# Half-height matmuls two at a time: scores and the last 64 rows of the low halves

## The chip, the cores and the metric

One core of a Trainium2 chip. The metric is the device time of one execution in microseconds (us). The kernel before took 1639.52 us, the median of three runs (1639.21 to 1640.65). Engines are named as in the profile: PE is TensorE's matmuls and PEld its weight loads, DVE is VectorE, ACT ScalarE, POOL GpSimd, SP the engine that issues the DMAs.

## The reference

The input x has 2048 rows of 576 columns. Two branches are mixed by a gate per row:

```
g = sigmoid((x * gate_w).sum(-1, keepdims=True))
a = infini_attention(x)              # 32 heads of 18 columns, 4 segments of 512 rows
b = (gelu(x @ w_gate) * (x @ w_up)) @ w_down     # hidden width 4608
out = g * a + (1 - g) * b
```

In a segment, each head has causal softmax attention over its 512 rows (`logits = q @ k.T * 18**-0.5 + mask`), mixed by a per-head sigmoid with a linear-attention memory of the segments before (`phi(q) @ M / (phi(q) @ z)`), and the result goes through `wo`. Everything is float32.

## The kernel before

**Precision.** A float32 matrix is scaled and split into two float16 parts, a high half and the low half that is left. A product is then three matmuls that add up in float32: high by high, high by low, low by high. The contraction of 576 is four chunks of 128 rows and a rest of 64. In the rest, the 64 rows of x stand twice, their high half in one half of the 128 partitions and the low half in the other, and the rows of the weights stand in both. So two full-height matmuls do the rest (`rest`, L1029 to L1032): the weights' high half by x's halves, and the weights' low half by x's halves.

**Two parts.** The projection part (0 to about 230 us) forms q, k, v and the memory's results, and leaves q and k in DRAM. Then 72 steps follow, two for each of the 36 tiles of 128 hidden columns of `w_gate` and `w_up`. The function `step(v)` writes one step out by hand in the order in which every engine executes it: nothing is scheduled later. A step does for one tile f = v // 2 and two of the four segments (c and e):

- the gate and up products of both segments, by a Strassen-like scheme with seven products instead of eight. They add up in the PSUM banks V, X (tagged G) and Y (tagged U); `product` issues six matmuls of 512 columns, `rest` two. `first_product` forms V, DVE copies V and X out and into Y, and the sums A11, A22, S1 to S4 and the rests G4 and U4 complete the gate and up values in turn;
- `gelu` on ACT, the multiplication by the up part on DVE (`hidden`), the split of the result into halves on ACT and POOL (`hidden_pair`);
- eight chains of the down product of the block before (`down`, L983, six matmuls of 288 columns each), into two PSUM banks tagged dn in turn; DVE adds each to the sum `acc` in SBUF (L991). A block is four steps, two tiles;
- attention of one head, in two units of one segment each, two steps behind (k = v - 2, for 64 steps): the scores (`score_piece`, L887) as matmuls of 512, 128, 384 and 256 columns into the two banks tagged st, the masking with a row maximum on DVE (L893), `powers` on ACT, `pair_rows` on ACT and POOL, a transposing DMA (`turn_rows`), and `values` (20 matmuls of 37 columns) in the next step;
- the weights of later tiles: scaling, sums and low halves on POOL (`scale_g`, `sums_g`, `low_g`, L250 to L283), high halves on ACT, the sums of squares that give the scales on DVE (`squares`, L80), and once a block `scales`, a small TensorE sum into a dn bank and six small DVE instructions.

q has two halves and k two halves too. A head's scores are one matmul with 72 rows (18 columns by four products of halves). Two 512-row loads per operand, repeated, lay these 72 rows out (`load_head`).

What sets the order around the change is the text of `step` alone: each engine executes its instructions in that order, and waits where a bank or a tile isn't free or ready.

## Time and profile before

| what | us |
|---|---|
| median of the runs | 1639.52 |
| the profiled execution | 1635.53 |
| its span in the trace | 1633.8 |
| PE busy | 1621.4 |
| DVE busy | 1268.9 |
| POOL busy | 1162.5 |
| ACT busy | 1081.3 |

The span is the time from the first instruction of the program to the last; the execution's own time is a little longer. In a row of the timeline the columns are the start and the duration in us, the engine, the line of the kernel, the operation, the tiles (out<-in), the shape (partitions x columns; 64*128 is a matmul that takes 64 of TensorE's 128 rows), the count, and in brackets the idle time before the row with what ended it. A row can merge like instructions that follow each other. In a row of a line or a tile three durations in ns stand for the shortest, the median and the longest. The mean granted TensorE clock was 1.0.

### The profile page before, as it was taken

The page shows a single profiled execution, that of the slowest core. Times are in us where ns is not written, and L with a number is a line of the kernel's source. Part 1 is how long each engine was busy: PE and PEld are TensorE (multiplying, and loading weights), DVE is VectorE, ACT ScalarE, POOL GpSimd, SP SyncE. Part 2 cuts the span into 40 slices and gives each one's busy share as a digit, 9 for nine tenths or more (in the row PEclk, how much of TensorE's full clock was granted, in tenths as well). Part 3 has the DMA queues.
Part 4 walks back from the last instruction along what each step waited for, and adds up shares of the span by engine and source line. Part 5 has one row for each costly group of instructions (what it writes and reads, how often), then busy time and mean ns, then how long its engine had stood idle before and what let it go on. Part 6 is the DMA issues. An engine that isn't in the chain of part 4 may idle for free.

```text
span 1633.8 us, 32332 instructions
## 1 busy us (share of the span) xinstructions
PE 1621.4 (99%) x11924; PEld 986.2 (60%) x11924; DVE 1268.9 (78%) x3140; ACT 1081.3 (66%) x1774; POOL 1162.5 (71%) x1057
## 2 busy tenths in 40 slices
PE   9999999999999999999999999999999999999999
PEld 5655754555665555665555665555665556665577
DVE  6576786888888888888887888888888888876643
ACT  6566447777777777777777777777767777763200
POOL 2233647888888889797978888897879797885300
PEclk9999999999999999999999999999999999999999
DMA  6532344776867686777766676777677575645351
GB/s 246 193 120 95 134 139 87 110 132 106 137 107 134 105 129 115 139 123 118 127 111 132 109 138 112 130 116 131 126 126 132 110 132 108 125 73 127 84 131 59
DMA packets 465502, 200.57 MB, mean 123 GB/s; under 512 B 425280, under 2 KB 434496, under 8 KB 464832
## 3 DMA queue, kind: packets, MB, share of 16 engines
q1 hardware_dynamic: 465344, 198.52, 62.0%
q8 instruction: 93, 1.52, 0.4%
q14 instruction: 65, 0.53, 0.1%
HBM read 82.60 MB, written 27.26 MB: 67 GB/s over the span
## 4 chain that ended last, share of the span: by engine, by line
PE 94%; DVE 3%; DMA 1%; ACT 1%; issue 1%; POOL 0%; SPq 0%; DVEq 0%; ACTq 0%; POOLq 0%
PE dn L983 25%; PE U L1025 17%; PE V L1025 11%; PE G L1025 11%; PE st L887 4%; PE pv L937 4%; PE V L1032 4%; PE st L312 3%; PE U L1032 2%; PE G L1032 2%; PE dn L312 2%; PE st L302 2%; PE G L302 1%; PE st L531 1%; PE U L302 1%
## 5 line engine op out<-in xcount | busy, mean ns | idle before, releaser
L983 PE MATMUL dn<-paird,hh 128*128 128x288 f16 x3402 | 486.7, 286 | 0.0
L1025 PEld LDWEIGHTS <-pairg 128*128 128x128 f16 x3024 | 290.2, 98 | 276.5 <-issue 5.0
L917 POOL TENSOR_TENSOR ph<-pf,ph 128x512 f16<-128x512 f32 (+1 forms) x256 | 373.8, 1460 | 79.5 <-ACT ph L916 41.0
L983 PEld LDWEIGHTS <-hh 128*128 128x128 f16 x3456 | 337.1, 98 | 137.9 <-issue 0.3
L991 DVE SCALAR_TENSOR_TENSOR acc<-dn,ev,acc 128x288 f32<-128x288 f32 x535 | 267.4, 512 | 66.5 <-PE dn L983 63.4
L906 ACT ACTIVATE pf<-pf,mb,esc 128x512 f32<-128x512 f32 (+3 forms) x512 | 293.0, 642 | 2.9
L1010 POOL TENSOR_TENSOR hh<-gl,hh 128x512 f16<-128x512 f32 x144 | 187.6, 1303 | 135.2 <-ACT hh L1009 135.2
L893 DVE CUSTOM_DVE_ANT_0 pf<-st,mask 128x512 f32<-128x512 f32 (+3 forms) x512 | 228.8, 483 | 67.5 <-PE st L887 67.5
L1025 PE MATMUL U<-xt,pairg 128*128 128x512 f16 x864 | 210.0, 379 | 1.9 <-DVE gl L1151 1.9
L1025 PE MATMUL G<-x,pairg 128*128 128x512 f16 x864 | 210.0, 379 | 0.0
L916 ACT ACTIVATE ph<-pf 128x512 f16<-128x512 f32 (+1 forms) x256 | 184.3, 720 | 0.0
L283 POOL TENSOR_TENSOR pairg<-raw,pairg 128x512 f16<-128x512 f32 (+2 forms) x144 | 167.0, 1179 | 8.3 <-ACT pairg L279 8.3
L1015 ACT ACTIVATE gl<-gl,sc 128x512 f32<-128x512 f32 x144 | 103.4, 718 | 80.4 <-DVE gl L1165 40.5
L903 ACT ACTIVATE mb<-mx,esc 128x4 f32<-128x4 f32 x128 | 37.1, 290 | 180.3 <-DVE mx L893 180.3
L1009 ACT ACTIVATE hh<-gl 128x512 f16<-128x512 f32 x144 | 89.6, 622 | 79.3 <-DVE gl L1005 79.3
L250 POOL TENSOR_SCALAR raw<-raw,sc 128x640 f32<-128x640 f32 x72 | 137.2, 1918 | 0.0
L887 PE MATMUL st<-kt,qt 72*128 72x512 f16 (+3 forms) x512 | 111.6, 299 | 0.6 <-DVE mx L893 0.6
L1025 PE MATMUL V<-x,pairg 128*128 128x512 f16 x432 | 105.0, 379 | 0.8 <-DVE gl L1125 0.8
L1025 PE MATMUL U<-x,pairg 128*128 128x512 f16 x432 | 104.8, 378 | 0.3 <-DVE gl L1165 0.3
L1025 PE MATMUL V<-xt,pairg 128*128 128x512 f16 x432 | 105.0, 379 | 0.0
L1015 ACT ACT_TABLE_LOAD x66 | 84.7, 1283 | 23.4 <-DVE gl L1152 22.6
L1032 PEld LDWEIGHTS <-pairg 128*128 128x128 f16 x576 | 56.3, 98 | 68.0
(260 smaller groups left out, 2532.3 us busy)
## 6 DMA issues: line engine op xcount, KB each, us to landing
raw<-in_wgu_dram SPq DMA_DIRECT2D x36, 640.0 KB
rawd<-in_wd_dram SPq DMA_DIRECT2D x36, 288.0 KB
qk<-stage SPq DMA_DIRECT2D x36, 256.0 KB
qt<-qk SPq DMA_DIRECT2D x128, 72.0 KB
kt<-qk SPq DMA_DIRECT2D x128, 72.0 KB
vp<-vstage SPq DMA_DIRECT2D x16, 296.0 KB
vt<-vp SPq DMA_DIRECT2D x16, 296.0 KB
orow<-oa SPq DMA_DIRECT2D x16, 288.0 KB
```

The lines of the kernel that those rows point to most:

```text
L283: pool.tensor_tensor(spot(f, *p, 1), raw_g[f][:, p[0] : p[1]], spot(f, *p, 0), OP.subtract)
L887: pe.matmul(o[:, off : off + n], q[:, e * L + qi * P : e * L + (qi + 1) * P], kt[:, e * L : e * L + n], start=True, stop=True)
L893: dve.tensor_tensor_reduce(prob[a][:, COL[qi] : COL[qi + 1]], o[:, off : off + n], mask[:, L - n :], 1.0, -3e38, OP.add, OP.max, mx[a][:, ...
L906: act.activation(r, r, AF.Exp, bias=b[:, qi : qi + 1], scale=esc[:, 0, c : c + 1])
L916: act.activation(h[:, 0, cols], p[:, cols], AF.Copy)
L917: pool.tensor_tensor(h[:, 1, cols], p[:, cols], h[:, 0, cols], OP.subtract)
L983: pe.matmul(o[:, :NH], hh[:, a, q * P : (q + 1) * P], w[:, b, n * NH : (n + 1) * NH], start=i == 0, stop=i == 5)
L991: dve.scalar_tensor_tensor(av, o[:, :NH], ev, av, OP.mult, OP.add)
L1010: pool.tensor_tensor(hh[:, 1], t, hh[:, 0], OP.subtract)
L1015: act.activation(t, o, AF.Gelu_apprx_tanh, scale=scl[f // 2][0][:, 2 + c : 3 + c])
L1025: pe.matmul(o, w[:, i, (a + k) * P : (a + k + 1) * P], x[:, b + k], start=start and k == 0 and i == 0 and b == h, stop=k == 1 and i == 1, ...
L1032: pe.matmul(o, w[:, i, a * P : (a + 1) * P], x[:, b], start=False, stop=i == 1, skip_group_check=True)
```

## The change

The scores drop the product of the two low halves: 54 rows instead of 72. The rows are laid out twice, in partitions 0 to 53 and 64 to 117. The matmul of 512 columns is issued in the first place, those of 384 and 128 in the second, and that of 256 in the first again, all four in a row; the last one's bank is now one of the two tagged dn.

The rests of the weights' low half lose their product with x's low half, so that 64 rows are left. x's halves are laid out the other way round for odd segments, so that the two segments' matmuls stand in different halves of TensorE's rows. They are issued in pairs by `low_rests`, for V and Y in the middle of a step and for X and Y at its end, each time directly ahead of a unit's scores. In the first block (fb == 0) the full-height form stays. The rest of V's first product moves: the sum for it (UG = U4 - G4) is formed once for the weights by `sums_g` instead of for x, so `first_product` has no rest, the fourth `form_sums` and its load go, and the weight tiles are 17 instead of 16 blocks wide.

Around this the order of a step changes: the hidden multiplication of both segments moves to the head of the next step (`end_pair`), scores are taken out of PSUM in pieces later (`puts`), squares and scales move behind the first of the three late down chains, and the three late chains stand together. A third `gl` buffer is added, and a head's load is eight DMAs instead of four.

```diff
     def sums_g(f):
+        g4, u4 = r[:, 4 * P : KW], r[:, KW + 4 * P :]
...
+        pool.tensor_tensor(g4, u4, g4, OP.subtract)
...
-            for i in range(2):
-                sp.dma_start(q[2 * DH * i : 2 * DH * (i + 1)], qk[:, r0 : r0 + DH, :])
-                sp.dma_start(kt[2 * DH * i : 2 * DH * (i + 1)],
-                             qk[i : i + 1, D + r0 : D + r0 + DH, :].to_broadcast([2, DH, HT]))
+            for a in (0, 64):
+                b, d = a + 2 * DH, a + 3 * DH
+                sp.dma_start(q[a:b], qk[:, r0 : r0 + DH, :])
+                sp.dma_start(q[b:d], qk[0, r0 : r0 + DH, :])
+                sp.dma_start(kt[a:b], qk[0:1, D + r0 : D + r0 + DH, :].to_broadcast([2, DH, HT]))
+                sp.dma_start(kt[b:d], qk[1, D + r0 : D + r0 + DH, :])
...
-        PIECES = ((3,), (0, 2), (1,))
+        PIECES = (((3,), 0), ((2, 0), 64), ((1,), 0))
+        def scores(a):
...
+            for qis, r in PIECES:
+                o = bank("dn", 2) if qis == (1,) else bank("st", 2)
+                spots, off, h = [], 0, slice(r, r + 3 * DH)
+                for qi in qis:
+                    n = (qi + 1) * P
+                    pe.matmul(o[:, off : off + n], q[h, e * L + qi * P : e * L + (qi + 1) * P],
+                              kt[h, e * L : e * L + n], start=True, stop=True)
...
+        def rest(o, f, a, x, parts=(0, 1)):
             w = pair_g[f]
+            for i in parts:
+                pe.matmul(o, w[:, i, a * P : (a + 1) * P], x[:, 8], start=False, stop=i == 1, skip_group_check=True)
+        def low_rests(f, *both):
+            for (o, a, x), h in zip(both, (slice(0, 64), slice(64, P))):
+                pe.matmul(o, pair_g[f][h, 1, a * P : (a + 1) * P], x[h, 8], start=False, stop=True, skip_group_check=True)
...
+        def end_pair():
+            for g in ends:
+                hidden(*g)
+            for f, c, o, g in ends:
+                hidden_pair(f, c, g)
+            ends.clear()
...
         def step(v):
...
+            end_pair()
...
+            product(Y, f, S1, t, 0, 2)
+            rest(Y, f, G4, x2_, (0,) if fb else (0, 1))
+            if fb:
+                low_rests(f, (V, G4, x1), (Y, G4, x2_))
+            if on(k):
+                puts[2 * k] = scores(2 * k)
...
             product(Y, f, S4, x2_, 2, 6)
+            rest(Y, f, UG, x2_, (0,) if fb else (0, 1))
             some(lb, late[:1])
+            if fb:
+                gate_squares(fb, i4, 1)
+                if i4 == 1:
+                    scales(fb + 1)
+                    scales_out(fb + 1)
...
             if done is not None:
                 result_low(done)
+            some(lb, late[1:])
+            if fb:
+                low_rests(f, (X, U4, x1), (Y, UG, x2_))
+                ends.append((f, c, X, g0))
+            if on(k):
+                puts[2 * k + 1] = scores(2 * k + 1)
+            ends.append((f, e, Y, g1))
```

More of the change, by code (lines that the diff above doesn't have):

```diff
@@ L261, in spot @@
         t = flat(pair_g[f])
-        o = o * P + part * 16 * P
+        o = o * P + part * GB * P
         return t[:, o : o + b - a]
@@ L1082, in first_product @@
             product(V, f, S3, xt[p], 8, 10, True)
-            rest(V, f, G4, x16[2 * p + 1], 8)
             return V
+        ends, puts = [], {}
+        def end_pair():
[4 more added lines that the diff above has]
+            ends.clear()
         def step(v):
@@ L1111, in step @@
             if on(k - 1):
+                powers(2 * k - 1)
+                pair_rows(2 * k - 1, 0)
                 pair_rows(2 * k - 1, 1)
@@ L1117, in step @@
             weights_load(fb, i4)
-            if done is not None:
-                result_high(done)
-            x1, x2_, t = x16[c], x16[e], xt[p]
-            there = v in ahead
-            V = ahead.pop(v) if there else first_product(v)
-            X, Y = bank("G"), bank("U")
-            g1 = gl_tile()
-            dve.tensor_copy(g1, V)
-            if not there:
-                scored(2 * k, 0)
-                scored(2 * k, 1)
-            product(X, f, A11, x1, 0, 4, True)
-            dve.tensor_copy(Y, X)
-            if there:
-                scored(2 * k, 0)
-                scored(2 * k, 1)
-            if v == 0:
-                last_sum(1, 1)
-            if v == 1:
-                scale_result()
-            some(fb - 1, early[:1])
             product(V, f, A22, x2_, 0, 4)
-            rest(V, f, G4, t, 12)
-            scored(2 * k, 2)
-            if on(k):
-                powers(2 * k)
+            rest(V, f, G4, x1, (0,) if fb else (0, 1))
             product(Y, f, S2, t, 4, 6)
```

187 lines of the change are left out of this document (89 added, 98 removed).

## The prediction

> **What bounds the kernel now.** I read the page's busy shares and its chain first, then TensorE's timeline over one pair of steps, then the stretches where TensorE already changes between 128 rows and 64, then DVE and POOL around the places that the change touches.
>
> ```profile
> span 1633.8 us, 32332 instructions
> PE 1621.4 (99%) x11924; PEld 986.2 (60%) x11924; DVE 1268.9 (78%) x3140; ACT 1081.3 (66%) x1774; POOL 1162.5 (71%) x1057
> PE 94%; DVE 3%; DMA 1%; ACT 1%; issue 1%; POOL 0%; SPq 0%; DVEq 0%; ACTq 0%; POOLq 0%
> ```
>
> TensorE is busy for 99% and is 94% of the chain that ends last. So the time is the length of TensorE's stream, plus every wait newly put into it. The stream of one whole step, from one first product of V to the next:
>
> ```profile
> 811.23 1.46 PE L1025 MATMUL V<-xt,pairg 128*128 128x512 f16 x6
> 812.52 0.59 PE L1032 MATMUL V<-x,pairg 128*128 128x512 f16 x2
> 812.96 0.60 PE L887 MATMUL st<-kt,qt 72*128 72x512 f16 x3
> 813.39 1.46 PE L1025 MATMUL G<-x,pairg 128*128 128x512 f16 x6
> ...
> 817.15 0.27 PE L887 MATMUL st<-kt,qt 72*128 72x256 f16 x1
> 817.26 1.46 PE L1025 MATMUL U<-xt,pairg 128*128 128x512 f16 x6
> 818.56 0.90 PE L983 MATMUL dn<-paird,hh 128*128 128x288 f16 x6
> 819.29 1.46 PE L1025 MATMUL G<-x,pairg 128*128 128x512 f16 x6
> ...
> 830.00 1.24 PE L1025 MATMUL V<-xt,pairg 128*128 128x512 f16 x5
> ```
>
> Durations include about 0.16 us of pipeline behind the streaming (six products take 1.46, the next group starts after 1.29), so costs are differences of starts: a 512-column matmul 0.216 us (1.29/6; two take 0.43), a down chain 0.73 (818.56 to 819.29), the scores' first three matmuls 0.43 (812.96 to 813.39) and the fourth 0.11. The step is 18.77 us.
>
> **What the change removes from the stream.** Each step has eight last-64-row matmuls of 512 columns (rest): 8 x 0.216 = 1.73. After it, in blocks past the first, four stay whole and four halves go out as two pairs, one half-matmul in rows 0 to 63 and the other in 64 to 127. Scores per unit: 512 and 128+384 columns side by side, then 256 alone. Whether halves run together is in the trace, since the value rows' fifth chunk is already done so:
>
> ```profile
> 13.83 0.65 PE L517 MATMUL V<-acc,raw 128*128 128x288 f32 x2
> 14.31 0.65 PE L517 MATMUL pv<-acc,raw 128*128 128x288 f32 x2
> ...
> 15.60 0.40 PE L517 MATMUL V<-acc,raw 64*128 64x288 f32 x1
> 15.60 0.40 PE L517 MATMUL pv<-acc,raw 64*128 64x288 f32 x1
> 15.84 0.40 PE L517 MATMUL V<-acc,raw 64*128 64x288 f32 x1
> ...
> 16.18 0.51 PE L517 MATMUL G<-acc,raw 128*128 128x290 f32 x1
> ```
>
> Full-height matmuls come every 0.24 us (13.83 to 14.31 for two); a pair of 64-row ones also takes 0.24 (15.60 to 15.84), its second starting within 0.01. So I take a pair as one matmul plus 0.007. Low halves: 1.73 - (4 x 0.216 + 2 x 0.223) = 0.42 us a step. Scores: 0.54 a unit becomes 0.22 + 0.11, so 0.21 saved, 0.43 for a step's two.
>
> **What the switches cost.** Each step now enters and leaves 64-row work at two places, four switches. In the fence above the last pair should be through at 15.84 + 0.24 = 16.08, and the next 128-row matmul starts at 16.18: 0.10 lost. Going in, from f16:
>
> ```profile
> 62.00 0.29 PE L315 MATMUL U<-wv,x 128*128 128x288 f16 x1
> 62.21 0.27 PE L559 MATMUL st<-ident,phi 64*128 64x64 f32 x1
> ```
> ```profile
> 229.94 0.60 PE L1025 MATMUL V<-xt,pairg 128*128 128x512 f16 x2
> ```
>
> 288 columns stream in 0.12, so 0.09 is lost. Weights can't be loaded ahead over a switch. In f32 that shows as 0.51 instead of 0.40 in the row at 16.18, 0.11 more; in f16 two products after a switch take 0.60 instead of 0.59, 0.01 more. The bounds are thus 0.09 and 0.21; I take 0.105, because all work at the new places is f16. Four switches: 0.42 us a step. The Trainium skill (TensorEngine Tiling (Array Packing), Key Properties) says that changing the tiling mode drains TensorE; it speaks against the change without a price, and the trace agrees, with 0.09 to 0.10.
>
> Net for the 62 steps with both parts (steps 4 to 65): 0.42 + 0.43 - 0.42 = 0.43, in all 26.5 us. Steps 2 and 3 (scores alone) and 66 to 71 (low halves alone) save what their switches cost: nothing.
>
> **What the new order makes TensorE wait for.** The down chains use two banks in turn. The last three (call them l0, l1, l2) now follow each other at the end of a step, with DVE's squares or scales ordered between l0's and l1's evictions, and the fourth score matmul now takes the bank of l1. The trace has this situation once, at the end of step 69:
>
> ```profile
> 1517.95 1.79 PE L983 MATMUL dn<-paird,hh 128*128 128x288 f16 x13
> 1518.28 0.52 DVE L991 SCALAR_TENSOR_TENSOR acc<-dn,ev,acc 128x288 f32<-128x288 f32 x1 [1.29 <-PE dn L983]
> ...
> 1519.37 0.93 DVE L991 SCALAR_TENSOR_TENSOR acc<-dn,ev,acc 128x288 f32<-128x288 f32 x2
> ...
> 1520.03 0.36 PE L85 MATMUL dn<-wst,ones 128*128 128x5 f32 x2 [0.28 <-DVE acc L991]
> ```
>
> A chain's bank is free 0.76 us after its last matmul has streamed (0.16 pipeline, 0.04 to DVE, 0.51 eviction, 0.05 back).
> - Every step: l2 wants l0's bank after 0.73: 0.04. Steps of the first and fourth kind (step number mod 4 is 0 or 3): 34 x 0.04 = 1.3.
> - Second kind: the scales' sum takes a bank between l0 and l1, so l1 wants l0's bank after the sum alone (0.13, by which such a step is longer before): it waits 0.63. 17 x 0.63 = 10.7. DVE's scales then delay l1's eviction. Their price before:
>
> ```profile
> 763.53 0.51 DVE L991 SCALAR_TENSOR_TENSOR acc<-dn,ev,acc 128x288 f32<-128x288 f32 x1
> 763.64 2.27 POOL L283 TENSOR_TENSOR pairg<-raw,pairg 128x512 f16<-128x512 f32 x2
> ...
> 764.15 0.67 DVE L211 TENSOR_SCALAR z<-x,z 128x4 f32<-128x4 f32 x1
> 764.85 1.08 DVE L215 TENSOR_SCALAR pb<-z 128x4 int32<-128x4 int32 x1
> 766.04 0.51 DVE L991 SCALAR_TENSOR_TENSOR acc<-dn,ev,acc 128x288 f32<-128x288 f32 x1
> ```
> ```profile
> L211 DVE TENSOR_SCALAR z<-x,z x19: 229/668/676, 174.3 to 1511.7; 128x4 f32<-128x4 f32 x19
> L215 DVE TENSOR_SCALAR pb<-z x19: 169/1079/1081, 174.6 to 1512.0; 128x4 int32<-128x4 int32 x19
> ```
>
> From eviction to eviction 2.51 us beside POOL's L283, of which both long ones are waiting (229 and 169 ns at their shortest): 1.2 without. With 1.2 the fourth score matmul finds its bank free; with 2.51 it waits 0.49 more.
> - Third kind: squares of 640 columns lie there:
>
> ```profile
> L80 DVE CUSTOM_DVE_ANT_0 junk<-raw x69: 810/1109/1898, 170.7 to 1428.5; 128x640 bf16<-128x640 f32 x69
> ```
>
> Counted from l0's end, l1's bank is free at 1.12 + the squares, and the fourth score matmul wants it at 2 x 0.73 + 0.04 + 0.105 + 0.22 + 0.22 = 2.05: it waits for what the squares take above 0.93. Between 0 (0.81 us) and 0.97 (1.90 us).
>
> Which price holds is POOL's place then. POOL's rows:
>
> ```profile
> 775.00 3.79 POOL L250 TENSOR_SCALAR raw<-raw,sc 128x640 f32<-128x640 f32 x2
> 778.77 1.72 POOL L287 TENSOR_SCALAR rawd<-rawd,sc 128x576 f32<-128x576 f32 x1
> ...
> 781.89 1.16 POOL L1010 TENSOR_TENSOR hh<-gl,hh 128x512 f16<-128x512 f32 x1
> 783.01 1.64 POOL L917 TENSOR_TENSOR ph<-pf,ph 128x768 f16<-128x768 f32 x1
> 784.62 2.27 POOL L283 TENSOR_TENSOR pairg<-raw,pairg 128x640 f16<-128x640 f32 x2
> 786.85 1.28 POOL L295 TENSOR_TENSOR paird<-rawd,paird 128x576 f16<-128x576 f32 x1
> ...
> 792.50 0.73 POOL L270 TENSOR_TENSOR raw<-raw 128x256 f32<-128x256 f32 x1
> ```
>
> In the new order the even unit's scores stand 6 us before a step's end, and POOL gets their probabilities last; with evictions, powers and copies ahead I estimate that it ends them 5 us into the next step. Behind them it does the hidden halves (2 x 1.16), the weights, the odd probabilities (1.16 for 512 columns, as for the hidden halves, + 1.64) and the low halves. l0 streams until 18.35 - 1.47 (l1, l2) - 0.76 (switches, pair, scores) = 16.1 us into its step, and DVE comes to the scales or squares 0.63 later, at 16.8. Second kind: 5.0 + 2.3 + 3.6 (sums: four of 0.73 and more, and the new one) + 2.8 + 2.5 = 16.2, clear of the scales. Third kind: 5.0 + 2.3 + 3.8 + 1.7 + 2.8 + 2.3 + 1.3 = 19.2, beside the squares. First kind: 5.0 + 2.3 + 3.8 + 2.8 + 2.3 = 16.2, clear. So I take 1.2 for the scales, and for third-kind squares 1.37, near the middle of their bounds: 0.44 x 15 = 6.6.
>
> Waits: 1.3 + 10.7 + 6.6 = 18.6 us, between 12 (no contention) and 48 (all at the long prices: 17 x 1.12 and 31 x 0.95).
>
> **What lies beside other work.** POOL gets one more subtraction and 128 more low-half columns for each of 36 weight tiles, about 0.37 + 0.26 us, 23 us on an engine with 470 us free; ACT some 4 us. A head's load is eight DMAs instead of four and half as many bytes again; the tiles are two steps ahead of use, and SP holds no work due sooner. The four form_sums of the last rows and their load go from the projection part, where TensorE is full: nothing. TensorE needs the transposed probabilities 11.9 us into the next step by the stream's order, POOL's part ends at 5: that leaves some 7 us for two transposes. A third gl buffer covers hidden halves that now end later; without it DVE's copy of U would wait for POOL. Start-up (steps 2 to 4) moves either way by up to 3 us: I take 0.
>
> **Sum.** -26.5 + 18.6 = -7.9 us. The profiled execution took 1635.5 us (span 1633.8): 1627.6 by it. The runs' median is 1639.5, 4.0 above: 1631.6 as a median.
>
> **Rivals.**
> 1. Slower, by DVE's place at the step's end: squares and scales run at the long prices because POOL is later than I count. Waits 48, so +21: 1661. For it: 19 scales had a median of 0.67 and 1.08. Against: POOL's sum ends before them in three kinds of four. It decides once waits pass 26.5 us.
> 2. Halves overlap only in part, or not (then the change doesn't do what it says). There are 264 pairs (68 x 2 and 128); the gain is gone at 0.03 us more for each, and without overlap 56 us come back: 1688. For it: the trace shows pairs in f32 alone, which streams half as fast. The Trainium skill (TensorE: Matmul & The Clock Gate, Measured speedup vs the span model) measured 3.07 for four row tiles of 512 columns; as an estimate, that efficiency would make a pair 0.28 us and the time 1647. No row shows it.
> 3. Switches cost 0.20 as in f32: 280 x 0.095 = 27 more, 1658. Against: the f16 row at 229.94.
> 4. Waits hidden (DVE ahead, banks free): only 26.5 less the small ones: 1614. For it: in the trace of before TensorE waits hardly at all. Against: three chains on two banks are a sum of rows.
>
> **How the numbers follow.** Forecast (waits of 14 to 23 us, 1627 to 1636) 0.38; rival 4 and its neighbourhood 0.20; between them and no change, within 0.2% (3.3 us, about what a measurement tells from no change) 0.14; rival 1 0.16, rival 2 0.06 (in part 0.04), rival 3 0.06. Faster 0.58, same 0.14, slower 0.28. The range goes from 1612 (rival 4) to 1660 (rivals 1 and 3, rival 2 by the estimate); the forecast's own is 1627 to 1636.
>
> **What would show it.** Pairs: U beginning within 0.01 us of V, next group 0.22 later. Switches: 0.10 between the stream's end and the next weights. Steady steps of 18.35 us in the first and fourth kind, 19.1 in the second, 18.9 in the third. TensorE waiting on DVE's acc eviction at a down chain and at the fourth score matmul. Wrong if starts of a pair lie 0.1 or more apart, or if those waits sum to over 26 us.

## The result, and the profile after

The changed kernel takes 1738.22 us (median of 5 runs, 1737.41 to 1739.14) against 1639.21 us before (5 runs): the ratio is 1.061, with a 95% interval from 1.059 to 1.062. It is 6% slower; the forecast was 1631.6.

The page of the changed kernel, its span, busy shares and the chain that ended last:

```profile
span 1736.5 us, 32603 instructions
PE 1631.3 (94%) x11924; PEld 942.7 (54%) x11924; DVE 1292.3 (74%) x3136; ACT 1089.8 (63%) x1770; POOL 1166.1 (67%) x1093
PE 51%; POOL 26%; ACT 10%; DVE 9%; issue 3%; DMA 0%; SPq 0%; POOLq 0%; DVEq 0%
```

Before, TensorE was busy for 99% and made up 94% of the chain. Now it stands still for 105 us, and 26% of the chain is POOL's. The view of TensorE's waits (who waited for what: us in total, times, longest) names them:

```profile
PE dn L982 <- POOL paird L301: 48.3, 16, 3.1
PE dn L982 <- DVE acc L990: 17.2, 30, 0.7
PE dn L982 <- DVE mx L892: 16.4, 16, 1.3
PE dn L884 <- DVE acc L990: 10.8, 14, 0.8
```

The first row is once per block (15 steps of the fourth kind and one in the start-up): a down chain waits for POOL to write the low half of the down weights (`low_d`, L301). TensorE's timeline at the end of a step of the fourth kind (step number mod 4 is 3) shows where; columns as before, idle time ahead of a row in brackets:

```profile
851.85 0.65 PE L982 MATMUL dn<-paird,hh 128*128 128x288 f16 x4
855.43 2.53 PE L982 MATMUL dn<-paird,hh 128*128 128x288 f16 x14 [2.93 <-POOL paird L301]
857.89 0.61 PE L1034 MATMUL G<-x,pairg 64*128 64x512 f16 x1
857.90 0.60 PE L1034 MATMUL U<-x,pairg 64*128 64x512 f16 x1
...
859.08 1.25 PE L1022 MATMUL V<-xt,pairg 128*128 128x512 f16 x3
```

And POOL's timeline at the same place:

```profile
847.24 1.72 POOL L293 TENSOR_SCALAR rawd<-rawd,sc 128x576 f32<-128x576 f32 x1
848.92 2.76 POOL L916 TENSOR_TENSOR ph<-pf,ph 128x512 f16<-128x512 f32 x2
851.64 2.50 POOL L289 TENSOR_TENSOR pairg<-raw,pairg 128x640 f16<-128x640 f32 x2
854.11 1.27 POOL L301 TENSOR_TENSOR paird<-rawd,paird 128x576 f16<-128x576 f32 x1
```

The late chain l0 starts with four matmuls that use ready weights, its fifth wants the low half at 852.3, and POOL ends L301 at 855.4. POOL isn't idle ahead of it; the instruction stands last in its queue. Behind the wait TensorE is also slower for a while: the pair at 857.89 takes 0.61 and 0.60 us instead of 0.39. The windows' last three columns are granted clock, DMA share and GB/s:

```profile
842.00:857.00 15.00, 12.07 (x92) 7.11 (x91) 8.98 (x22) 12.64 (x20) 13.14 (x13) 0.99 0.96 158
857.00:859.00 2.00, 2.00 (x11) 0.58 (x8) 1.46 (x4) 1.02 (x2) 1.64 (x2) 0.50 0.95 260
859.00:863.00 4.00, 4.00 (x26) 2.05 (x26) 2.94 (x6) 1.26 (x2) 4.00 (x4) 0.88 0.98 116
```

The first steps (mod 4 is 0) have two more waits, for DVE. TensorE's rows, then DVE's:

```profile
872.72 0.90 PE L982 MATMUL dn<-paird,hh 128*128 128x288 f16 x6 [0.67 <-DVE acc L990]
874.62 0.90 PE L982 MATMUL dn<-paird,hh 128*128 128x288 f16 x6 [1.01 <-DVE mx L892]
```
```profile
868.12 2.68 DVE L950 SCALAR_TENSOR_TENSOR osum<-osum,gha,ord 128x72 f32<-128x72 f32 x2
870.84 1.40 DVE L954 TENSOR_TENSOR ob<-ob,osum 128x144 f32<-128x144 f32 x1
872.16 0.51 DVE L990 SCALAR_TENSOR_TENSOR acc<-dn,ev,acc 128x288 f32<-128x288 f32 x1
```

The eviction at 872.16 stands behind the end of the normalization, which takes 4.1 us here beside POOL's L916 and L289. Other steps show 0.50 and 0.31 for the same instructions.

The work that the change is about went as forecast. TensorE's rows at the first place:

```profile
808.93 0.38 PE L1029 MATMUL U<-x,pairg 128*128 128x512 f16 x1
809.24 0.39 PE L1034 MATMUL V<-x,pairg 64*128 64x512 f16 x1
809.24 0.39 PE L1034 MATMUL U<-x,pairg 64*128 64x512 f16 x1
809.47 0.38 PE L884 MATMUL st<-kt,qt 54*128 54x512 f16 x3
809.69 0.27 PE L884 MATMUL dn<-kt,qt 54*128 54x256 f16 x1
809.89 0.67 PE L936 MATMUL pv<-vt,pt 128*128 128x37 f16 x20
```

The two halves start together, and the next matmuls follow 0.23 us later, for two. Going in costs 0.31 - 0.216 = 0.09 us, coming out 0.20 - 0.11 = 0.09.

The step lengths below are counted from one first product of V to the next in each timeline, as medians over the 15 or 16 blocks; "first" is step number mod 4 = 0. Each run has its own letter and its section below; "ratio" is against the kernel before in the same comparison. A median hides single long steps; where they matter, the text gives means.

| kernel | us | ratio | 95% interval | first | second | third | fourth |
|---|---|---|---|---|---|---|---|
| before | 1639 | 1 | | 18.78 | 18.91 | 18.87 | 18.78 |
| forecast | 1631.6 | | | 18.35 | 19.1 | 18.9 | 18.35 |
| changed | 1738.2 | 1.061 | 1.059-1.062 | 20.49 | 19.09 | 19.29 | 22.87 |
| A: down weights early | 1698.7 | 1.038 | 1.035-1.040 | 20.95 | 19.09 | 19.37 | 19.16 |
| B: idle filled | 1734.3 | 1.058 | 1.053-1.063 | 20.61 | 19.09 | 19.37 | 21.61 |
| C: A, SP in order | 1698.3 | 1.037 | 1.034-1.040 | 18.35 | 21.70 | 19.39 | 19.17 |
| D: C, scales apart | 1738.2 | 1.061 | 1.059-1.062 | 20.49 | 24.34 | 18.36 | 18.84 |
| E: C, all loads late | 1833.6 | 1.118 | 1.116-1.120 | 28.27 | 19.09 | 21.88 | 18.65 |
| F: E and D | 1857.0 | 1.132 | 1.129-1.134 | 27.70 | 18.70 | 23.90 | 18.83 |
| G: changed, full height | 1747.6 | 1.066 | 1.064-1.068 | 20.57 | 19.54 | 18.91 | 23.51 |
| H: C, vt and ob moved | 1658.9 | 1.012 | 1.010-1.013 | 18.35 | 19.09 | 19.30 | 19.15 |
| I: H and D | 1685.4 | 1.028 | 1.026-1.029 | 20.51 | 18.88 | 18.36 | 18.85 |
| J: I, scaling on ACT | 1668.6 | 1.018 | 1.016-1.020 | 20.34 | 18.49 | 19.79 | 18.40 |
| K: J, normalization late | 1700.7 | 1.038 | 1.037-1.040 | 19.00 | 21.80 | 20.19 | 18.52 |
| L: K, full height | 1686.4 | 1.029 | 1.028-1.031 | 19.13 | 20.07 | 20.13 | 18.82 |
| M: J, two waits mended | 1630.2 | 0.994 | 0.993-0.996 | 18.35 | 18.77 | 18.71 | 18.45 |
| N: M, full height | 1677.8 | 1.023 | 1.021-1.025 | 18.80 | 18.94 | 20.70 | 18.82 |

### The profile page after: what moved, and what is told of

Its sections match the earlier page's. It is cut to its first block, busy times and chain, and to the rows that moved or that the text cites. A ratio compares the mean times of both kernels' runs of the same rounds, so it can differ in the third digit from the quotient of the medians.

```text
span 1736.5 us, 32603 instructions
## 1 busy us (share of the span) xinstructions
PE 1631.3 (94%) x11924; PEld 942.7 (54%) x11924; DVE 1292.3 (74%) x3136; ACT 1089.8 (63%) x1770; POOL 1166.1 (67%) x1093
## 4 chain that ended last, share of the span: by engine, by line
PE 51%; POOL 26%; ACT 10%; DVE 9%; issue 3%; DMA 0%; SPq 0%; POOLq 0%; DVEq 0%
PE dn L982 12%; POOL ph L916 7%; PE U L1022 7%; PE V L1022 6%; PE G L1022 5%; POOL hh L1009 4%; POOL raw L254 3%; POOL rawd L293 3%; ACT pf L905 3%; PE st L318 3%; PE st L308 2%; ACT L905 2%; POOL pairg L289 2%; PE dn L318 2%; PE G L308 2%
## 5 line engine op out<-in xcount | busy, mean ns | idle before, releaser
L982 PE MATMUL dn<-paird,hh 128*128 128x288 f16 x3402 | 499.4, 292 | 83.1 <-POOL paird L301 48.3
L916 POOL TENSOR_TENSOR ph<-pf,ph 128x512 f16<-128x512 f32 (+1 forms) x256 | 353.4, 1401 | 269.9 <-ACT ph L915 250.4
L1022 PEld LDWEIGHTS <-pairg 128*128 128x128 f16 x3024 | 286.0, 98 | 328.2 <-issue 45.1
L1009 POOL TENSOR_TENSOR hh<-gl,hh 128x512 f16<-128x512 f32 x144 | 172.1, 1215 | 54.8 <-ACT hh L1008 54.7
L289 POOL TENSOR_TENSOR pairg<-raw,pairg 128x640 f16<-128x640 f32 (+2 forms) x144 | 184.4, 1302 | 10.6 <-ACT pairg L285 10.6
L892 DVE CUSTOM_DVE_ANT_0 pf<-st,mask 128x512 f32<-128x512 f32 (+2 forms) x384 | 184.0, 504 | 0.0
L915 ACT ACTIVATE ph<-pf 128x512 f16<-128x512 f32 (+1 forms) x256 | 172.4, 720 | 0.0
L285 ACT ACTIVATE pairg<-raw 128x640 f16<-128x640 f32 (+2 forms) x144 | 88.2, 648 | 116.4 <-POOL raw L279 74.2
L1152 DVE COPY gl<-U 128x512 f32<-128x512 f32 x72 | 49.8, 692 | 88.5 <-PE U L1022 65.7
L1008 ACT ACTIVATE hh<-gl 128x512 f16<-128x512 f32 x144 | 84.8, 620 | 48.9 <-DVE gl L1004 48.3
L1175 DVE TENSOR_TENSOR gl<-U,gl 128x512 f32<-128x512 f32 x72 | 49.6, 689 | 64.1 <-PE U L1034 56.8
```

The costliest lines, as they stand in the source:

```text
L285: act.activation(spot(f, *p, 0), raw_g[f][:, p[0] : p[1]], AF.Copy)
L289: pool.tensor_tensor(spot(f, *p, 1), raw_g[f][:, p[0] : p[1]], spot(f, *p, 0), OP.subtract)
L892: dve.tensor_tensor_reduce(prob[a][:, COL[qi] : COL[qi + 1]], ov, mask[:, L - (qi + 1) * P :], 1.0, -3e38, OP.add, OP.max, mx[a][:, qi : q ...
L915: act.activation(h[:, 0, cols], p[:, cols], AF.Copy)
L916: pool.tensor_tensor(h[:, 1, cols], p[:, cols], h[:, 0, cols], OP.subtract)
L982: pe.matmul(o[:, :NH], hh[:, a, q * P : (q + 1) * P], w[:, b, n * NH : (n + 1) * NH], start=i == 0, stop=i == 5)
```

## The experiments

**A. The low half of the down weights earlier in the fourth step.**

```diff
             if i4 == 3:
-                sums_g(n0 + 2)
                 if fb:
                     scale_d(n0 + 1)
+                sums_g(n0 + 2)
...
                 powers(2 * k - 1)
+            if i4 == 3 and fb:
+                high_d(2 * fb + 1)
+                low_d(2 * fb + 1)
+            if on(k - 1):
                 pair_rows(2 * k - 1, 0)
```

> The changed kernel, but in the fourth step of a block POOL scales the last down weights first and forms their low half ahead of the odd unit's probabilities, so that it stands before the late down chains. Theory A (that wait, and what follows from it, is the whole surprise): the 48.3 us wait of the down chains for POOL's paird goes, the half clock behind it too (0.5 for 3.4 us, 16 times, about 1.7 us each), and the first step after it comes down from 20.3 to 21.0 us to about 18.4, since DVE's normalization was late through the same shift: 48 + 27 + 30 = 105 us less, near 1634. Rival B (the first step's loss has its own cause, POOL's new order beside DVE): only the fourth step gains, 4.6 us each, 16 times: 74 us less, near 1665. Rival C (POOL is short of time in every step, so the wait moves to another of its results): less than 40 us less.

The wait for paird went from 48.3 us to one of 4.3 in the start-up, and the fourth step lost 3.7 us. But the time fell by 40 us only. That is the bound that rival C gave, and its mechanism came: another late result took the first steps' time. TensorE's waits now:

```profile
PE pv L936 <- DMA pt<-ph: 31.2, 29, 2.2
PE dn L884 <- DVE acc L990: 21.0, 29, 0.9
PE dn L982 <- DVE acc L990: 7.8, 16, 0.5
PE dn L982 <- POOL paird L301: 4.3, 1, 4.3
```

So POOL's late low half is shown to cost the fourth step what the trace says, and the odd unit's transposed probabilities, wanted early in the next step, are the next late result.

**B. The idle time of the fourth step filled** with 14 matmuls of 512 columns whose result nobody reads (3.0 us).

```diff
+            if i4 == 3 and fb:
+                o = bank("V")
+                for _ in range(14):
+                    pe.matmul(o, pair_g[f][:, 0, :P], x1[:, 0], start=True, stop=True)
             some(lb, late[:1])
```

> The changed kernel with 14 useless matmuls of 512 columns (3.0 us of TensorE's stream) put ahead of the late down chains in every fourth step but the first, writing a bank that is free there, so that TensorE works instead of waiting 2.9 to 3.1 us for POOL's paird. The computation is otherwise whole. If the half clock behind the wait is a consequence of TensorE standing still, the clock stays at 1.0, the fourth step goes from about 22.9 us to 21.5 although TensorE does 14 matmuls more, and the run takes some 25 us less than the changed kernel. If the clock falls for another reason, the time is the same or up to 10 us longer.

3.0 us more work made the fourth step 1.26 us shorter: the half clock behind it is gone in 14 of 15 of them, and the wait itself has room for the work. The half clock is thus a consequence of the wait, not a cost of the pairs. The time moved little, by 4 us instead of 25 (1727.6 and 1741.0 us in two runs; the profile is of the longer one). In it the fourth steps give back 15 us, but seven first steps now have a stretch at half clock behind their waits of 0.68 and 1.01 us (8.5 us), and two steps in which nothing had waited, 67 and 71, are longer by the added work (6 us).

**C. A, and SP's transfers in the order of the code.** In the changed kernel the text of `step` binds PE, ACT, DVE and POOL, and the transfers are ordered by the scheduler.

```diff
-        with tc.manual_schedule(engines=ORDERED):
+        with tc.manual_schedule(engines=ORDERED | {mybir.EngineType.SP}):
```

> As the run with the early down weights, and SP issues the steps' DMAs in the written order, so that a unit's two transposing DMAs stand ahead of the results' stores and the next loads instead of behind up to eight of them. Theory A: the 31.2 us in which the values waited for transposed probabilities, all in the first step of a block, come from SP's queue alone; the first step falls from 19.6 to 24.0 us to about 18.5, and with it the half clock that these waits brought: about 42 us less than the run before, near 1657. Rival B: the probabilities themselves are late there (POOL ends them too late); the first step stays above 19.5 us and the run gains less than 15 us.

The first step came to 18.35 us, exactly the stream of the forecast, but the second rose to between 20.2 and 23.9 in 15 of 16 blocks, and the time stayed where A had it. SP's queue, then TensorE at the head of that step (which starts at 935.18):

```profile
931.34 0.39 SPq L860 DMA_DIRECT2D vt<-vp  x1
931.77 1.32 SPq L865 DMA_DIRECT2D ob<-om  x1
933.20 9.48 SPq L922 DMA_TRANSPOSE pt<-ph  x4
```
```profile
940.09 0.19 PE L936 MATMUL pv<-vt,pt 128*128 128x37 f16 x1 [1.41 <-DMA pt<-ph]
941.67 0.65 PE L936 MATMUL pv<-vt,pt 128*128 128x37 f16 x19 [1.39 <-DMA pt<-ph]
```

The transposes stand behind eight transfers of the next head and the loads of vt and ob. POOL had the low half ready at 931.2.

**D. C, with the scales of the second step and the second squares of the third put back into the middle of their steps.**

```diff
             some(fb - 1, early[1:2])
+            if fb and i4 == 1:
+                scales(fb + 1)
...
             some(fb - 1, early[2:3])
+            if i4 == 2 and fb:
+                gate_squares(fb, 2, 1)
...
-                gate_squares(fb, i4, 1)
+                if i4 == 0:
+                    gate_squares(fb, i4, 1)
                 if i4 == 1:
-                    scales(fb + 1)
                     scales_out(fb + 1)
```

> As the run with SP in order, and DVE's work is taken from between the evictions of the last three down chains: the scales go back to the second early down chain, where the kernel before has them, and the third step's second squares go behind the third early chain. By the bank sums of the prediction the second step falls from 19.09 to about 18.5 us and the third from 19.37 to about 18.4: 9 + 15 = 24 us less than the run with SP in order, near 1633, and then the whole is a few us faster than the kernel before. If DVE has no time at the new places either, the waits move there and less than 10 us are gained.

The third step lost its local wait (18.36 us), but the run was 40 us slower than C: the second step rose to 24.3, with waits for the transposes of 39.7 us in all, the half clock took 1.9 us more of a second step on average, and the first steps waited 16.6 us for POOL's low half of the gate weights. That shorter steps ask sooner for the same late results is how I read it; no run tests it alone.

**E. C, with the loads behind the transposes:** the weights' loads at the end of their step, vt and ob at the end of the first step of a block. **F. E and D together.**

```diff
-            weights_load(fb, i4)
...
+            weights_load(fb, i4)
             load_head(k + 2)
-            if v == 0:
-                load_v(0)
-            if i4 == 3:
-                load_v(fb + 1)
+            if i4 == 0:
+                load_v(fb)
```

> The kernel with early down weights and SP in the order of the code, with two things moved on SP's queue: the loads of the next weights stand behind the transposes of their step (they waited there for a buffer that POOL frees, up to 6.9 us in one row, and held the even unit's transposes back), and the loads of vt and ob for the next four heads stand one step later, behind the first step of a block instead of behind the fourth. Theory (the second step's wait for transposed probabilities is SP's queue: transposes stand behind loads that wait for a buffer, and beside the 1.2 MB of ob): the second step goes from 20.3 to 23.9 us back to 19.1, first, third and fourth stay at 18.35, 19.4 and 19.17, the row of the values' wait for pt goes from 29 us to under 5, and 1698.3 us become 1645 to 1660. Rival (POOL is what is late: the odd unit's low half ends only 4 us ahead of the step that wants it, wherever SP's loads stand): the second step stays above 20.5 us, the time above 1680.

> The same with the scales of the second step and the second squares of the third step put back into the middle of their steps, as tried before beside the late transposes (1738 us). Theory (the local waits for an eviction behind the scales and the squares go, and this time no transpose is late): second step 18.4 to 18.9, third 18.4, fourth 18.9, first 18.35; against the run with the loads moved alone 25 to 35 us less, 1615 to 1630 us, under the kernel before. Rival (DVE, ACT or POOL then are the next late ones, as in the try before): the first or second step is above 19.5 us and the time above 1645 us.

The second step went back to 19.09 us as the theory had it. But the first is ten us longer than in C, which gives the transposes more time too, so only H below shows that SP's order makes them late. The times are the worst of all: the raw gate weights now came after DVE wanted them. DVE in E:

```profile
913.80 0.83 DVE L81 CUSTOM_DVE_ANT_0 junk<-raw 128x640 bf16<-128x640 f32 x1 [10.85 <-DMA raw<-in_wgu_dram]
914.55 0.69 DVE L1155 COPY gl<-U 128x512 f32<-128x512 f32 x1
```

The squares waited 10.9 us, and the copy of U behind them, which nothing but the queue kept back, held up TensorE (up to 8.4 us, 144.9 in all). In F this wait is 153.2 us: the second step fell by 0.4 us, but the third, which D had shortened, rose to 23.90. Nothing else follows from F.

**G. The changed kernel's order with full height at both places** (72-row scores and 128-row low halves, one after the other, both with the low-by-low product again).

```diff
-            for (o, a, x), h in zip(both, (slice(0, 64), slice(64, P))):
-                pe.matmul(o, pair_g[f][h, 1, a * P : (a + 1) * P], x[h, 8], start=False, stop=True, skip_group_check=True)
+            for o, a, x in both:
+                pe.matmul(o, pair_g[f][:, 1, a * P : (a + 1) * P], x[:, 8], start=False, stop=True, skip_group_check=True)
```

> The changed kernel's order with matmuls of full height at the same two places: scores from 72 rows one after the other, low halves of the last 64 rows from 128 rows one after the other, heads loaded by eight transfers as in the changed kernel. Nothing runs two at a time, TensorE's tile size never changes. Theory (the loss is the order: POOL's and SP's results late; the pairs gain what they should): no gain and no loss of the pairs, so 0.43 us more in each second and third step and at most that in the first and fourth, where POOL's wait takes it up: 1745 to 1765 us, 7 to 27 above the changed kernel, with the fourth step at 22 to 23.5 us as before. Rival (the pairs themselves cost, by switches or by two matmuls in each other's way): 1738 us or less, towards 1700.

9.4 us slower than the changed kernel, as the theory had it, and 108 slower than the kernel before: the new order alone makes the loss, and the pairs give a little of it back. TensorE waits 45.1 us for POOL's low half here too, and 15.2 us in the row of the scores' maxima. The second step shows the pairs' worth, 19.54 against 19.09; where a wait ends last, their gain goes into the wait. The third step is even 0.38 us shorter at full height: its squares (L81), which a chain's eviction waits for, take 1.34 us there and 1.85 in the changed kernel.

**H. C, with only vt and ob moved** behind the odd unit's transposes of the first step.

```diff
                 turn_rows(2 * k - 1)
+            if i4 == 0 and fb:
+                load_v(fb)
...
-            if i4 == 3:
-                load_v(fb + 1)
```

> The kernel with early down weights and SP in the order of the code, with one thing moved: vt and ob for the next four heads are loaded in the first step of their block, behind the transposes of the odd unit, instead of at the end of the fourth step, ahead of them. The weights' loads stay where they were (put behind the even unit's transposes they came 11 us too late for the squares that read them). Theory (the second step waits for transposed probabilities because vt and ob, 1.7 us of SP and 1.2 MB of transfer, stand ahead of the odd unit's transposes: 933.2 instead of 931.3, and 4.8 us for the first of them instead of 1.3): second step 19.1 us instead of 22.1, the others as they were (18.35, 19.4, 19.17), 1698.3 - 16 x 3.0 = 1645 to 1660 us. Rival (the eight transfers of the heads and the four of the result hold SP back by themselves): second step 20.3 us or more, over 1670 us.

1658.9 us, as expected: 79 of the 99 us are back with the low half of the down weights, SP's order and these two loads. TensorE's waits:

```profile
PE dn L884 <- DVE acc L990: 20.4, 29, 0.9
PE pv L936 <- DMA pt<-ph: 9.2, 10, 1.8
PE dn L982 <- DVE acc L990: 8.3, 17, 0.5
```

**I. H and D together.**

> The same, and the scales of the second step and the second squares of the third put back into the middle of their steps, as in the try of 1738 us. Theory (that try lost in its second step to the same late transposes, and gained 1.0 us in the third and 0.3 in the fourth): first step 18.35, second 18.5 to 19.0, third 18.4, fourth 18.85, 74.1 to 74.6 us a block against 75.3 before: 1618 to 1635 us, faster than the kernel before. Rival (with those waits gone POOL's halves are what comes late, as its 16.6 us of waits in the first step of that try say): first step 20.4 us, 1650 us or more.

The rival came: the third step is 18.36 us again, but the first waits for POOL's low half of the gate weights (16.6 us in all, 1.5 at most), and DVE waits 99 us for POOL's hidden halves. The second step is 20.48 us in the mean, from 18.48 to 24.34. POOL's queue is the limit of this order.

**J. I, with the scaling of the raw weights on ACT.**

```diff
-            pool.tensor_scalar(r, r, scl[f // 2][0][:, 0:1], None, OP.mult)
+            act.activation(r, r, AF.Copy, scale=scl[f // 2][0][:, 0:1])
...
-        pool.tensor_scalar(r, r, scl[f // 2 + 1][0][:, 1:2], None, OP.mult)
+        act.activation(r, r, AF.Copy, scale=scl[f // 2 + 1][0][:, 1:2])
```

> The kernel with early down weights, SP in the order of the code, vt and ob behind the transposes and the scales and squares in the middle of their steps (1685 us), with the scaling of the raw gate, up and down weights (two instructions of 1.87 us and up to two of 1.7 us of POOL, lines L254 and L293) on ACT instead, where a copy of 128x640 took 0.74 us. Theory (POOL's queue is what is late: low half of the gate weights 1.5 us late in the first step, the odd unit's low half late for the transposes that the second step wants, and both waits are followed by the half clock): POOL's queue gets some 11 us shorter in a block of 76, first step 18.35 us, second 18.5 to 19.0, third 18.4, fourth 18.85; 1618 to 1635 us, faster than the kernel before. Rival (ACT, lengthened by 4.4 us a block and ahead of the odd unit's powers, makes the same results late): first or second step over 19.5 us, 1650 us or more.

17 us less than I, but 1668.6 misses the theory; the rival's numbers came, its cause, a late ACT, did not. TensorE waits for POOL and for transposes only once each (3.1 and 1.8 us), and the second and fourth steps are at 18.49 and 18.40 us. But the third has a wait of 1.26 us, since DVE's copy of U waits 2.17 us for POOL's hidden halves, which stand behind the scales' six small operations, and the first has the two waits of the changed kernel again (0.67 and 1.01 us). DVE there:

```profile
1142.87 2.69 DVE L950 SCALAR_TENSOR_TENSOR osum<-osum,gha,ord 128x72 f32<-128x72 f32 x2
1145.59 1.40 DVE L954 TENSOR_TENSOR ob<-ob,osum 128x144 f32<-128x144 f32 x1
1146.91 0.51 DVE L990 SCALAR_TENSOR_TENSOR acc<-dn,ev,acc 128x288 f32<-128x288 f32 x1
```

POOL, freed of the scaling, starts L916 at 1142.71, just ahead of L950; in I they missed each other in this step, and L950's two took 0.52 us.

**K. J, with those two operations behind the first late eviction in the first and third step,** and the six small POOL operations of the scales (`scales_out`) behind the third step's hidden halves. **L. K at full height.**

```diff
+                if i4 % 2:
+                    normalize_out(2 * k - 3)
...
             some(lb, late[:1])
+            if on(k - 2) and i4 % 2 == 0:
+                normalize_out(2 * k - 3)
...
             end_pair()
+            if i4 == 2 and fb:
+                scales_out(fb + 1)
```

> The kernel of 1668.6 us (down weights early, SP in the order of the code, vt and ob behind the transposes, scales and squares in the middle, scaling on ACT), with the last two operations of the normalization (L950, two of 72 columns that took 2.69 us beside POOL instead of 0.50, and L954, 1.40 instead of 0.31) moved behind the first late eviction in the first and third step, and POOL's six small operations of the scales (2.3 us) moved behind the hidden halves of the third step. Theory (what is left, 1.6 us in the first step and 1.3 in the third in the rows of the scores' maxima, is the eviction of the third chain, late behind these operations in DVE's queue): first step 18.4 us instead of 19.7 to 20.3, third 18.4 instead of 19.8, second 18.5 and fourth 18.4 as they are: 73.7 us a block against 75.3 before, 1615 to 1630 us, faster than the kernel before. Rival (the eviction is late for other reasons, POOL's hold on DVE's operations moves to the next of them): first or third step above 19.2 us, 1645 us or more.

> The same kernel with matmuls of full height at both places (scores from 72 rows one after the other, low halves of 128 rows one after the other). Theory (pairs and switches are worth what the prediction said, 0.85 - 0.42 = 0.43 us in each of 62 steps, wherever nothing else waits): 20 to 28 us above the run before it, 1640 to 1655 us, steps of 18.8 us. Rival (the pairs are worth less once DVE and POOL set the pace): 10 us or less above it.

Both theories failed. In the second step, where nothing had been moved, DVE's normalization now met POOL, and its eviction came 2.2 us late:

```profile
1186.08 2.62 DVE L959 SCALAR_TENSOR_TENSOR osum<-osum,gha,ord 128x72 f32<-128x72 f32 x2
1188.73 1.39 DVE L963 TENSOR_TENSOR ob<-ob,osum 128x144 f32<-128x144 f32 x1
```

In the first step the moved operations stand 0.80 us ahead of l1's eviction, and the fourth score matmul waits 0.48; in the third they meet POOL at their new place too (2.7 us), and it waits 1.66. At full height the second step's wait is 0.78 instead of 2.2, and L is even faster than K; a pair of runs whose waits differ so much doesn't price the pairs.

**M. J, with the two operations at the end of the first step alone,** where POOL has 9 us free, and `scales_out` ahead of the second step's even probabilities, where POOL waits 3.8 us for ACT. **N. M at full height.**

```diff
+                if i4:
+                    normalize_out(2 * k - 3)
...
+            if fb and i4 == 1:
+                scales_out(fb + 1)
             if on(k):
                 powers(2 * k)
...
             some(lb, late[1:])
+            if on(k - 2) and i4 == 0:
+                normalize_out(2 * k - 3)
```

> From the kernel of 1668.6 us (scaling on ACT), where only two waits are left: 0.67 and 1.01 us in the first step (third chain's eviction behind the normalization's last two operations, 2.69 and 1.40 us beside POOL) and 1.26 us in the third (behind a copy that waits 2.17 us for POOL's hidden halves, which stand behind six small operations of the scales). Those two operations of the normalization move to the end of the first step alone, where POOL is idle for 9 us; the six small ones move ahead of the even unit's probabilities of the second step, into 3.8 us in which POOL waits for ACT. Theory (single late results, no bound by DVE and POOL together): first step 18.4 us instead of 20.3, third 18.4 to 18.8 instead of 19.8, second 18.5 and fourth 18.4 as they are; 1668.6 - 16 x 1.7 - 15 x 1.2 = 1623, 1615 to 1632, faster than the kernel before. Rival (DVE and POOL in each other's way are the bound: what is moved away here is late elsewhere): one of the steps over 19.3 us, 1645 us or more.

> The same with matmuls of full height at both places. Theory (the pairs gain 0.43 us a step net of switches where nothing waits): 62 x 0.43 = 27 us above the run before it, 18 to 30, steps of 18.8 us. Rival: under 10 us above it, or below it as at 1686 against 1701 us.

M takes 1630.18 us, 0.994 of the kernel before (0.993 to 0.996): a small gain, but clear of the interval, and the only version that beats both kernels. Its page and TensorE's largest waits:

```profile
span 1630.4 us, 32481 instructions
PE 1605.8 (98%) x11924; PEld 933.5 (57%) x11924; DVE 1285.0 (79%) x3136; ACT 1160.5 (71%) x1878; POOL 984.8 (60%) x985
```
```profile
PE dn L991 <- POOL paird L301: 4.3, 1, 4.3
PE dn L991 <- DVE mx L892: 3.7, 15, 1.1
PE dn L991 <- DVE acc L999: 3.4, 3, 1.8
```

It lies within the expected range, 7 us above its middle sum of 1623, mostly by the second step (18.77, and in two blocks over 20). N is 48 us above it, more than expected: some 30 of them in the third step (15 x 2.0), where waits for DVE came back (16.2 us in the row of the scores' maxima). The clean measure of the pairs is the first step, in which neither kernel waits: 18.35 against 18.80 us.

## Why the prediction was wrong

**TensorE's own stream: right.** A pair as one matmul, switches at 0.09 to 0.10, a net gain of 0.43 us a step: first steps of 18.35 us in C, H and M, and 18.80 - 18.35 = 0.45 between N and M. Rivals 2 and 3 fall with it. The efficiency measured on the Trainium skill's page TensorE: Matmul & The Clock Gate (Measured speedup vs the span model) would have given, as an estimate, 0.28 us for a pair, and the trace shows 0.23; the drain that TensorEngine Tiling (Array Packing), Key Properties, names is there, with 0.09.

**Waits at the step's end: second kind right, third and fourth short.** The second step was forecast at 19.1 and took 19.09; the scales ran at their short price (L214 and L218 0.23 and 0.17 us), since POOL was clear of them, as counted. The third was forecast at 18.9 and took 19.29. That POOL would be beside the squares was counted right, but their price, taken near the middle of its bounds as 1.37 us, was 1.85 in all 15 blocks, the long end. By the prediction's own sum the wait is then 1.85 - 0.93 = 0.92 us instead of 0.44; the trace has 0.76 of it as idle time, the rest is the pipeline behind the streaming. POOL, DVE and TensorE there:

```profile
833.61 2.85 POOL L289 TENSOR_TENSOR pairg<-raw,pairg 128x640 f16<-128x640 f32 x2
833.85 1.84 DVE L81 CUSTOM_DVE_ANT_0 junk<-raw 128x640 bf16<-128x640 f32 x1
836.18 0.27 PE L884 MATMUL dn<-kt,qt 54*128 54x256 f16 x1 [0.76 <-DVE acc L990]
```

For the fourth I gave 0.04; H, where POOL's wait is gone, shows 19.15, because `result_low`'s subtraction (L966) stands between l0's and l1's evictions as the squares do. The list of what lies there in each kind had left it out. It costs that much only beside POOL's L289: in H it takes 1.77 us, in J 0.97, and J's fourth step is 18.40 without a wait. H's rows:

```profile
821.05 3.03 POOL L289 TENSOR_TENSOR pairg<-raw,pairg 128x640 f16<-128x640 f32 x2
821.30 1.77 DVE L966 SCALAR_TENSOR_TENSOR oh<-ob,wsc,oh 128x576 f16<-128x576 f32 x1
```

Rival 1 named this mechanism, and by the prediction's own sign it was there: the waits for DVE sum to 46 us, over 26. But at 6 us for the third kind and 12 for the fourth (15 blocks by 0.4 and 0.8) it isn't the loss. The largest row, 48.3 us for POOL, stands in no term, no rival and no sign; slower had a chance of 0.28, and no rival went past 1688.

**The step that failed: "What lies beside other work".** It costed POOL's and SP's share at nothing, by POOL's total (470 us free) and by "SP holds no work due sooner". POOL's order was worked out for one question alone, whether it runs beside DVE's scales and squares, and so for the second, third and first kind. The same sum for the fourth kind was never made. It is 5.0 + 2.3 + 3.6 (sums) + 1.7 (scaling) + 2.8 (odd probabilities) + 2.5 (gate weights) + 1.3 (down weights) = 19.2 us into the step, while l0, which streams until 16.1, wants the down weights' low half two matmuls of 0.12 before its end, at 15.9. That is 3.3 us late. In the trace POOL ends 19.0 us into the step, TensorE wants the result at 16.0, and its idle time is 2.93. Every number stood in the prediction, and the consumer wasn't asked for.

**Where the 107 us lie.** Against the forecast's step lengths the fourth steps are 15 x 4.4 = 66 us longer (means over the blocks), the first 16 x 2.2 = 35, the third 6, and the start-up (steps 0 to 3) is 3.4 us longer than before: together 110. By the profiled execution, 1738.2 against 1627.6, the forecast was 110.6 short.

- The fourth steps' 66 us are POOL's late low half and the half clock behind it (A and B): 45 us of idle time and, by the clock records, some 20 lost at half clock. Of the 4.4 us of a step A leaves 0.8, which are `result_low`'s.
- The first steps' 35 us are the two waits behind the normalization (26 us of idle time and some 5 for the pipeline that runs empty at each) and the rest of the half clock (some 4). G has the same waits, so they are the order's, not the pairs'. That they come from POOL's L916 beside L950 is read from rows of the changed kernel, I, J and K (2.62 to 2.69 us where they meet, 0.52 where they don't); J brought the waits back by moving L916, and M took them away by moving L950.
- With those gone, the odd unit's transposes come late (A, C), and SP's order is why (H). The forecast's "7 us for two transposes" was for the even unit; the odd one's values, moved from the end of a step to the head of the next, were not looked at. That nothing is scheduled later holds for the four compute engines only: SP's transfers were not in the order of `step` (C).

**The other terms.** The start-up moved by 3.4 us, outside my 3. Rival 4 (1614) needs all banks free, and M, which comes nearest to that, ends at 1630: three kinds of step are still 0.1 to 0.4 us above the stream of 18.35, single blocks are over 20, and its start-up is as long as that of the changed kernel. That M comes within 1.4 us of the forecast is luck and doesn't make the forecast right: M is another kernel, with work moved from POOL to ACT and six things reordered.

## What to carry to other kernels

When a change moves work on an engine that is not the bound, make that engine's queue a sum for each kind of step and ask of every result in it who wants it and when; spare time in total says nothing. After one wait is mended expect the next to be near: five of the ten mended versions here were slower than the one they came from, and the one that beat both kernels put its last two moves where the trace showed POOL idle.

## What the runs showed of the hardware

- TensorE's granted clock fell to 0.50 for 3.41 us (the trace's clock records) after it had stood still for 2.93 us; so it was in 14 of the 15 fourth steps of the changed kernel, and in one of 15 where B filled the idle time, behind another wait of 2.97. So a wait of 3 us costs up to 1.7 us more behind it. Shorter waits did the same in some blocks and not in others: in B waits of 0.68 and 1.01 us in seven of 16 first steps, in K one of 2.2 us in seven second steps of 14 (and 1.00 behind the one at 1190.61), in C two of 1.4 us within 3 us (0.62 from 943 to 947). In each run the stretches at half clock begin whole multiples of 3.41 us apart, so where on that grid a wait falls seems to decide; no run moves a wait along it. The Trainium skill (TensorE: Matmul & The Clock Gate, Part 1) puts the half clock after an idle window of about 3.4 us that runs freely; the length and the grid agree with these records, but here less idle than a whole window was enough.
- DVE's small operations with two operands in SBUF took as long as POOL's two-operand ones beside them: in J the two of L950 took 2.69 us and L954 1.40, beside POOL's L916 with 2.75 for two; alone they take 0.50 and 0.31. Longer ones were held up too (L81 1.84 and L966 1.77 us beside L289, 0.82 and 0.81 elsewhere); the evictions, which read PSUM, stayed at 0.51 beside L289 (at 872.16). The Trainium skill (SBUF — State Buffer, SBUF: two separate sides) describes a port pair that the two engines share and hold for a whole instruction; these rows agree. For the small ones the cost is set by POOL's instruction, not by DVE's, so a DVE operation that takes 0.3 us alone can be the dearest in its queue.
